# A list of steps in another order: the steps from the 120th on are re-ordered, and 117 of them change between VectorE and GpSimd

## The chip, the core and the metric

The kernel runs on one core of one Trainium2 chip. The metric is the device time of one execution in microseconds, as the median of several executions. In the profile the engines are called PE (TensorE, the matrix engine), DVE (VectorE), ACT (ScalarE), POOL (GpSimd) and SP (SyncE, which here issues the DMA transfers). All arithmetic is in 32-bit floats.

## The reference

The kernel computes a Mamba2 state-space layer and behind it a SwiGLU feed-forward layer. The first has batch 4, 8 heads, 768 positions, head dimension 32 and state 16, in 24 chunks of 32 positions:

```python
for c in range(nc):
    ...
    L = np.exp(cum[:, :, :, None] - cum[:, :, None, :]) * causal
    M = np.einsum('bhin,bhjn->bhij', Cc, Bc) * L
    y[:, :, sl] = np.einsum('bhij,bhjd->bhid', M, xc) \
        + np.einsum('bhin,bhnd->bhid', Cc, state) * np.exp(cum)[:, :, :, None]
    state = decay_full[:, :, None, None] * state + np.sum(Bx, axis=2)
```

Its result, as 3072 tokens of 256 numbers, goes through the second, with d_ff = 1536:

```python
xn = x / np.sqrt(np.mean(x * x, axis=-1, keepdims=True) + 1e-06) * rms_g
g = xn @ w_gate
return (g / (1.0 + np.exp(-g)) * (xn @ w_val) @ w_out).astype(np.float32)
```

## The kernel before

The 3072 tokens are cut into six blocks of 512. A block runs through the state-space layer (two pairs of chunk groups per block), the norm, the products with the gate and value weights, the product of SiLU(gate) and value (`hid`), and the product with the output weights. While PE makes the feed-forward products of one block, the other engines prepare the state-space part of the next.

Nothing is ordered by a scheduler. The program is a list of 1725 steps, written as one long string (`order`) at the end of the kernel. A loop reads it from the first to the last step and calls one small function for each; that function emits its instructions, each on a fixed engine. So the list sets the order on each engine, and each engine runs its own instructions in that order, waiting on semaphores for the others. A step reads `block:kind.numbers/banks`. A kind that ends in p (`hidp`, `hidgp`, `up`, `txp`, `cwp`, `twop`, `subp`, `scalep`, `scale2p`) is the same step on POOL instead of DVE.

The kinds that matter below, with the lines of the profile on which their instructions stand:

- `fetch.k` (L184): SP loads a piece of raw weights, 511.5 KB, into one of six buffers `wr`. `pow` (ACT), `man` (L224, DVE) and `wt` (L230, DVE) turn it into weights.
- `rowe` (L1196) stores decays to DRAM, `rowout` (L1189) row sums, `dT.p` (L566) loads the decays back, spread over partitions, and `Td.p` (L573, DVE) multiplies by them. `g` and `gg` (L592, L599, PE) are the products of C and B that come next; `L` and `L1` (L632 and on, DVE) multiply them by the decays, `y` (L705, L734, PE) are the layer's outputs.
- `spread` (L500, SP), `sub`/`subp` (L506) and `ex` make the decay matrix `L`; `ex` is an exponential on ACT and two causal selects on POOL (L493).
- `ms`, `rs`, `rb` are the sums and roots of the norm, `xn` (L873, DVE, two instructions) applies it; `tx`/`txp` (L954) make differences of it.
- `early` and `gate` (L901, L891, PE) are the first block's first feed-forward products. `P.k.j` (L977, PE) are the others: seven products for four, in the manner of Strassen; `take` (L983, ACT) and `C` (L989, DVE) combine them, `silu` is ACT's, `hid`/`hidp` (L1002) multiplies.
- `u.n`/`up.n` (L1076) are sums and differences of parts of `hid`, `cw` (L946) and `two` (L1054) the same of weights, for the output product `O.k.h` (L1108, PE), which uses 20 products with such sums. `w.n` (L1139, DVE, or ACT) adds its parts into `ob`, and `put` (SP) stores the result.

Of the kernel before, what the change touches and what calls it, by code (L numbers as in the profile page):

```python
# [20 lines left out]
def kernel(  # L21
# [1255 lines left out]
    def of_chunk(n, fn):  # L1277
# [45 lines left out]
        0:L1.2.2 0:fetch.8 0:fetch.9 0:silu.2 0:hid.2 0:man.8 0:pow.8 0:wt.8 0:L1.2.3 0:gate.3/2
        0:pow.7 0:gate.4/1 0:fetch.6 0:man.6 0:A.2 0:txp.0.1 0:silu.3 0:x.3 0:hid.3 0:pow.6
        0:gate.5/0 0:tx.0.2 0:txp.0.3 0:fetch.11 0:wt.7 0:man.9 0:fetch.10 0:S.2 0:silu.4 0:pow.9
        0:fetch.12 0:hid.4 0:bc.5 0:wt.6 0:cwp.3.0 0:wt.9 0:silu.5 0:hid.5 0:man.11 0:cw.3.1
        0:cw.3.2 0:cw.4.0 0:fetch.13 0:silu.1 0:y.2/2 0:S.3 0:x.5 0:cwp.4.1 0:ydone.0 0:switch.1
        0:P.2.3 0:bc.4 0:x.4 0:switch.0 0:pow.11 0:P.1.3 0:P.1.4 0:take.1.3 0:C.11.3 0:P.2.4 0:P.6.3
        0:yt.2 0:sq.2 0:gg.3/2 0:take.1.4 0:silug.11.3 0:C.11.4 0:L.3.0 0:take.6.3 0:cwp.3.3 0:P.5.3
        0:cwp.1.0 0:P.7.3 0:silug.11.4 0:P.6.4 0:take.7.3 0:P.5.4 0:P.4.3 0:hidgp.11.3 0:wt.11  # L1330
        0:L1.3.2 0:scale.5 0:L1.3.3 0:cwp.4.2 0:cwp.4.3 0:take.6.4 0:C.22.3 0:P.3.3 0:man.10
        0:scale.4 0:pow.10 0:wt.10 0:silug.21.3 0:cwp.5.0 0:cwp.5.1 0:hidg.11.4 0:P.7.4 0:take.7.4
        0:y.3/2 0:C.12.3 0:fetch.15 1:table 0:silug.22.3 0:hid.1 0:P.4.4 0:pow.12 0:silug.21.4
        0:hidg.21.3 0:spread.10 0:spread.9 0:P.1.5 0:spread.11 0:silug.12.3 0:C.22.4 0:P.2.5
# [6 lines left out]
        0:up.0 0:u.3 0:pow.15 0:wt.15 0:o.2 0:o.3 0:o.4 0:o.5 0:xn.1 1:P.2.0 1:P.1.1 1:P.1.0
        0:fetch.16 0:man.16 0:pow.16 0:sq2.2.1.3 0:sq2.2.1.0 0:sq2.2.1.2 0:tx.1.0 0:u.1 0:tx.1.2
        0:u.2 0:pow.17 0:wt.16 0:wt.17 1:twop.2 1:twop.1 1:two.0 1:cwp.2.2 0:O.16 0:O.2 0:O.0 0:oc.0
        0:silug.12.4 0:oc.1 1:take.1.0 0:C.12.5 0:tx.1.1 1:P.6.0 1:take.6.0 0:silug.12.5 1:C.11.0
        1:silu.11.0 0:O.4 1:P.5.0 1:two.3 1:two.8 1:two.11 1:two.9 0:tx.1.3 0:u.9 1:P.7.0 1:take.1.1
        1:P.6.1 0:O.15 0:ex.11 1:P.2.1 0:w.2 0:O.17 0:w.3 0:hidg.12.5 0:O.6 1:take.7.0 1:take.6.1
        1:P.7.1 1:C.11.1 1:P.5.1 1:silu.11.1 1:take.7.1 0:w.5 0:w.6 0:w.0 1:spread.0 1:spread.2
        0:sq2.2.1.1 1:two.5 1:T.0.1 1:twop.7 0:O.3 0:w.4 0:w.10 0:up.4 0:cwp.1.3 0:ydone.3 1:P.4.1
        1:silu.21.1 0:u.5 0:hidg.12.4 1:hid.21.1 1:C.22.0 0:w.1 1:hid.11.0 1:P.4.0 1:silu.21.0
        0:up.6 0:hidgp.22.5 0:u.7 0:up.8 1:cw.2.1 1:C.22.1 0:O.9 0:u.10 1:Tt.0.1 1:P.1.2 1:take.1.2  # L1350
        0:O.18 0:w.8 0:O.8 1:P.3.0 1:C.12.0 1:silu.12.0 1:hid.21.0 0:w.9 1:silu.22.1 1:P.6.2
        1:take.6.2 1:Tt.0.0 1:P.3.1 1:P.2.2 1:twop.4 0:O.7 0:up.13 1:hidp.22.1 1:twop.6 0:ex.9
        1:cwp.2.3 1:hid.11.1 0:w.7 1:two.10 0:u.11 0:u.12 0:O.13 1:T.1.1 0:w.20 1:Tt.1.1 0:w.14
        0:w.15 1:P.7.2 1:take.7.2 0:O.12 1:P.1.3 0:O.11 1:P.4.2 0:w.16 1:C.11.2 1:hid.12.0 0:w.13
        0:w.22 0:u.14 0:w.18 0:w.11 0:O.5 1:take.1.3 1:P.6.3 0:O.14 1:silu.11.2 1:Tt.1.0 1:spread.3
        0:spread.8 1:sub.3 1:ex.3 1:dT.1 0:sq2.2.0.1 0:sq2.2.0.3 3:bc.0 0:sq2.2.0.2 1:C.12.1 0:w.12
        1:T.0.0 1:hid.11.2 0:O.1 0:w.19 0:u.15 1:T.1.0 0:O.19 1:P.5.2 1:P.2.3 1:sq2.1.0 1:sq2.1.1
        1:dT.0 1:sq2.0.3 1:sq2.1.2 1:sq2.0.0 1:sq2.0.2 0:w.21 0:w.17 0:w.23 0:w.24 0:O.10 1:scale2.0
        0:w.25 0:put.2 1:spread.1 0:put.0 0:put.3 0:put.1 1:sq2.1.3 1:take.6.3 1:P.7.3 1:silu.21.2
        1:g 1:C.22.2 1:take.7.3 1:P.4.3 1:Td.1 1:C.11.3 0:sub.10 1:hid.21.2 1:silu.22.2 0:table.0  # L1360
        1:silu.12.1 1:hidp.12.1 1:silu.22.0 1:hidp.22.0 1:hidp.22.2 0:sub.8 1:P.3.2 1:C.12.2
        1:silu.11.3 1:silu.21.3 0:ex.8 1:P.1.4 1:take.1.4 0:ex.10 1:subp.2 1:hid.21.3 1:P.5.3
        1:C.22.3 1:P.2.4 1:C.11.4 1:silu.11.4 1:hid.11.4 1:P.6.4 1:take.6.4 1:silu.22.3 1:P.3.3
        1:P.1.5 1:silu.12.2 3:table 1:take.1.5 1:hidp.12.2 1:C.12.3 1:silu.12.3 1:P.7.4 1:take.7.4
# [12 lines left out]
        1:O.14.0 1:O.5.0 1:O.14.1 2:scale2.0 1:O.5.1 1:w.7 1:w.22 1:u.14 1:w.8 1:O.19.0 1:O.19.1
        1:u.15 1:O.10.0 1:O.10.1 1:xn 2:P.1.1 1:tx.0 1:txp.2 2:take.1.1 1:w.14 1:txp.1 1:w.25 1:w.19
        1:w.17 1:w.23 1:w.15 1:tx.3 1:w.24 2:Td.1 2:P.1.0 2:take.1.0 2:P.2.0 2:P.6.1 2:C.11.0
        2:P.6.0 1:ex.2 1:ex.0 1:ex.1 2:sq2.1.2 2:spread.2 2:sq2.0.0 2:sq2.0.3 2:sq2.0.1 2:spread.0  # L1380
        1:w.21 1:put.2 2:sq2.1.3 2:P.2.1 2:C.11.1 2:L1.3 2:take.6.1 2:P.7.1 2:take.6.0 2:P.7.0
        2:take.7.0 0:exps 2:P.5.0 2:L1.2 2:C.22.0 2:L 2:P.5.1 2:take.7.1 2:P.4.0 2:silu.21.0
        2:silu.11.1 2:silu.11.0 2:silu.22.0 2:hid.11.0 2:C.22.1 2:P.3.0 2:C.12.0 2:hid.21.0 2:P.4.1
        2:silu.21.1 2:hid.21.1 2:subp.3 2:ex.3 2:y 2:hidp.22.0 2:P.1.3 2:take.1.3 2:subp.0 2:sq
        2:P.1.2 2:take.1.2 2:P.3.1 2:C.12.1 2:silu.12.1 2:hid.11.1 2:hidp.12.1 2:P.6.3 2:P.2.2
        2:take.6.3 2:silu.22.1 3:T.1.1 2:C.11.2 2:P.2.3 2:C.11.3 2:sq2.0.2 3:T.1.0 2:silu.11.3
        2:P.6.2 2:take.6.2 2:P.7.3 2:hid.22.1 2:P.5.3 2:take.7.3 2:C.22.3 3:T.0.0 2:x.1 2:spread.1
        2:hid.11.3 3:Tt.1.1 2:silu.22.3 2:hidp.22.3 2:P.7.2 2:P.5.2 2:take.7.2 2:silu.11.2 2:C.22.2
# [130 lines left out]
```

## Time and profile before

| | |
|---|---|
| median of three runs | 387.2 us (386.33 to 387.54) |
| the profiled execution | 387.79 us, of which the span of instructions is 386.0 us |
| granted clock of TensorE | 1.00 |
| PE busy | 379.9 us, 98% of the span |
| DVE, ACT, POOL busy | 282.1, 219.7, 152.3 us |
| moved by DMA | 28.04 MB |

The share of an engine is its busy time over the span. A list of waits says for which producer an engine stood still, and the chain of waits follows the work that ended last backwards to its start. A row of a timeline gives the start, the busy time, the engine, the line, the instruction and its operands, and in brackets how long the engine idled ahead of it and who released it. Rows of equal instructions that follow each other are joined (x12).

### The profile page before, as it was taken

How to read it: one execution, taken by the hardware profiler on the slowest of the kernel's cores; microseconds unless marked ns; L12 is line 12 of the kernel's file. 1: busy time of each engine (PE TensorE's matmuls, PEld its weight loads, DVE VectorE, ACT ScalarE, POOL GpSimd, SP SyncE). 2: the span in 40 equal slices, each digit the busy share in tenths (PEclk: the TensorE clock that was granted, in tenths of full speed). 3: DMA queues.
4: the chain of work that ended last, by engine and by line, in shares of the span. 5: the costliest groups of instructions: out<-in, count | busy, mean ns of one | idle time of the engine just before them, and what ended most of it. 6: DMA issues, size and time to landing. Idle time of an engine off the chain costs nothing.

```text
span 386.0 us, 9707 instructions
## 1 busy us (share of the span) xinstructions
PE 379.9 (98%) x3837; PEld 330.1 (85%) x3837; DVE 282.1 (73%) x632; ACT 219.7 (57%) x455; POOL 152.3 (39%) x171
## 2 busy tenths in 40 slices
PE   8999999999999999999999999999999999999997
PEld 5675478889988999888898988899888899888996
DVE  6895979999997989656688566578735677454675
ACT  2778767957698361776571446562474551555410
POOL 5022046536756554553475501463630046112131
PEclk9999999999999999999999999999999999999999
...
DMA packets 110084, 28.04 MB, mean 73 GB/s; under 512 B 94840, under 2 KB 107992, under 8 KB 110040
## 3 DMA queue, kind: packets, MB, share of 16 engines
...
## 4 chain that ended last, share of the span: by engine, by line
PE 92%; DMA 3%; DVE 1%; SPq 1%; ACT 1%; issue 1%; DVEq 0%
PE gate L977 30%; PE o L1108 23%; PE val L977 22%; PE y L734 3%; PE gate L891 3%; PE o L1009 3%; PE g L599 1%; DMA rowe<-e_sb 1%; PE gate L901 1%; DMA dT<-rowe 1%; PE e L460 1%; PE g L592 1%; DMA L<-rowd 1%; SPq L143 0%; PE idle L328 0%
## 5 line engine op out<-in xcount | busy, mean ns | idle before, releaser
L989 DVE TENSOR_TENSOR c<-val,p 128x512 f32<-128x512 f32 x99 | 67.6, 687 | 39.1 <-PE val L977 30.3
L983 ACT COPY p<-gate 128x512 f32<-128x512 f32 x99 | 56.9, 582 | 49.7 <-PE gate L977 46.6
L977 PE MATMUL gate<-tx,wgv 128*128 128x256 f32 x264 | 65.8, 380 | 0.0
L977 PEld LDWEIGHTS gate<-tx,wgv 128*128 128x128 f32 x264 | 49.4, 190 | 6.7 <-ACT p L983 0.2
L1002 POOL TENSOR_TENSOR hid<-c 128x256 f32<-128x256 f32 x31 | 24.3, 795 | 76.4 <-ACT c L208 73.7
L208 ACT ACTIVATE c<-c 128x256 f32<-128x256 f32 x99 | 39.0, 414 | 25.4 <-DVE c L989 25.1
L1108 PE MATMUL o<-two,hid 128*128 128x128 f32 x308 | 42.4, 276 | 0.0
L1139 DVE TENSOR_TENSOR ob<-ob,o 128x128 f32<-128x128 f32 (+1 forms) x116 | 31.1, 295 | 14.0 <-PE o L1108 9.6
L1108 PEld LDWEIGHTS o<-two,hid 128*128 128x128 f32 x308 | 39.1, 192 | 1.1 <-ACT ob L1135 0.2
L1002 DVE TENSOR_TENSOR hid<-c 128x256 f32<-128x256 f32 x68 | 30.1, 455 | 7.9 <-ACT c L208 7.5
L977 PE MATMUL val<-tx,sw 128*128 128x256 f32 x132 | 33.9, 381 | 0.0
L977 PE MATMUL val<-xn,sw 128*128 128x256 f32 x132 | 33.9, 379 | 0.0
L977 PE MATMUL val<-xn,wgv 128*128 128x256 f32 x132 | 33.5, 380 | 0.0
L977 PE MATMUL gate<-xn,wgv 128*128 128x256 f32 x132 | 33.2, 381 | 0.0
L977 PE MATMUL gate<-tx,sw 128*128 128x256 f32 x132 | 33.1, 379 | 0.0
L1076 POOL TENSOR_TENSOR s<-s,hid 128x512 f32<-128x512 f32 (+1 forms) x14 | 18.1, 1291 | 28.3 <-PE o L1108 24.8
L493 POOL TENSOR_SCALAR_AFFINE_SELECT L<-L 64x512 f32<-64x512 f32 x32 | 22.0, 686 | 14.8 <-ACT L L208 13.7
L977 PEld LDWEIGHTS val<-xn,wgv 128*128 128x128 f32 x132 | 24.9, 190 | 3.4
L977 PEld LDWEIGHTS val<-tx,sw 128*128 128x128 f32 x132 | 24.6, 190 | 3.7 <-issue 0.4
L977 PEld LDWEIGHTS gate<-tx,sw 128*128 128x128 f32 x132 | 24.8, 190 | 3.2
L1002 DVE TENSOR_TENSOR hid<-u,gate 128x256 f32<-128x256 f32 x33 | 13.6, 417 | 18.5 <-ACT u L208 18.5
L1076 POOL TENSOR_TENSOR s<-hid 128x512 f32<-128x512 f32 (+1 forms) x15 | 19.6, 1310 | 18.5 <-DVE hid L1002 14.3
...
## 6 DMA issues: line engine op xcount, KB each, us to landing
...
wr<-in_moe_w_out_dram SPq DMA_DIRECT2D x6, 511.5 KB, 5.3
...
wr<-in_moe_w_gate_dram SPq DMA_DIRECT2D x5, 511.5 KB, 4.5
wr<-in_moe_w_val_dram SPq DMA_DIRECT2D x5, 511.5 KB, 5.6
...
```

Source lines behind the costliest of these rows:

```text
L208: nc.scalar.activation(**operands)
L493: nc.gpsimd.affine_select(out=L[r], in_=L[r], pattern=[[0, L.shape[1]], [1, HC]], compare_op=ALU.is_ge, fill=0.0, base=0, channel_multipli ...
L734: nc.tensor.matmul(out=y[2 * k + u][rows, (2 * n + i) * HC:(2 * n + i + 1) * HC], start=(k, u, rows.start) not in opened, stop=True, skip_ ...
L891: nc.tensor.matmul(out=gv[:, k], lhsT=w[:, t, fs], rhs=xns[0][:, t], start=(t == 0), stop=(t == 1))
L977: nc.tensor.matmul(out=dst[:, half[w]], lhsT=lhsT, rhs=rhs, start=(k in (1, 2, 5) and w == 0), stop=True, skip_group_check=True)
L983: nc.scalar.copy(out=t, in_=Xs[j])
L989: nc.vector.tensor_tensor(out=t, in0=Zs[j], in1=a, op=ALU.add)
L1002: engine.tensor_tensor(out=hid[:, 2 * j + c // 10 - 1, c % 10 - 1], in0=u, in1=src[:, half[1]], op=ALU.mult)
L1009: nc.tensor.matmul(out=o, lhsT=hid[:, f, k // 2, (k % 2) * P:(k % 2 + 1) * P], rhs=wo[:, f], start=opens, stop=(f == NF // 2 - 1), skip_gr ...
L1076: engine.tensor_tensor(out=hidden_or_sum(o)[:, g], in0=hidden_or_sum(in0)[:, g], in1=hidden_or_sum(in1)[:, g], op=ALU.add if in1[0] == "+" ...
L1108: nc.tensor.matmul(out=Os[blk, b][:, place * P:(place + 1) * P], lhsT=hidden_or_sum(u)[:, g], rhs=rhs, start=(blk, b) not in opened, stop= ...
L1139: nc.vector.tensor_tensor(out=o, in0=o, in1=src, op=ALU.add if what[0] == "+" else ALU.subtract)
```

## The change

Only the string `order` differs. The first 119 steps are the same; from the 120th on the same 1725 steps stand in another order, and 117 of them change their engine: 63 go from DVE to POOL (34 `hid`, 9 `u`, 5 `tx`, 4 `cw`, 4 `sub`, 6 `scale`, 1 `two`) and 54 from POOL to DVE (22 `u`, 16 `hid`, 7 `cw`, 5 `tx`, 2 `two`, 2 `sub`). The string is one line longer, so lines behind it move by one. Two lines of before and two of after:

```diff
-        0:early.1.0/1 0:early.1.1 0:dT.3 0:man.4 0:table.1 0:x.2 0:norm.1 0:man.5 0:Td.3 0:silu.0
...
-        2:O.13.0 2:O.13.1 2:ex.2 3:L 2:up.11 2:O.11.0 3:sq2.0.3 2:rb 2:xn 2:w.9 2:O.11.1 3:P.1.0
...
+        0:man.7 0:pow.4 0:wt.4 0:Tt.2.0 0:pow.7 0:fetch.9 0:fetch.8 0:dT.3 0:Td.3 0:wt.7 0:fetch.6
...
+        2:ex.2 3:L 3:L1.3 2:O.13.0 2:O.5.0 2:O.13.1 2:up.11 2:O.5.1 2:O.11.0 2:O.11.1 3:sq2.0.3 2:rb
```

On SP, in the first block, a piece of the difference from the store of the decays (`rowe.0`) to the loads of x:

```order
 L1196 DMA rowe<-e_sb 4x32x128
 L1189 DMA rowd<-r_sb 128x2x64
-L184 DMA wr<-in_moe_w_val_dram 128x2x1023
+L184 DMA wr<-in_moe_w_val_dram 128x2x1023 x2
+L184 DMA wr<-in_moe_w_gate_dram 128x2x1023
 L566 DMA dT<-rowe 128x1x256
-L150 DMA xr<-in_x_dram 128x8x32 x2
-L184 DMA wr<-in_moe_w_gate_dram 128x2x1023
-L184 DMA wr<-in_moe_w_val_dram 128x2x1023
```

Ahead of `dT.3` stood one load of weights; now there are three, `fetch.9` and `fetch.8` with it, and the loads of x have moved behind.

On POOL, at the end of block 2's feed-forward work, before:

```order
L1076 TENSOR_TENSOR s<-hid 128x512
L1076 TENSOR_TENSOR s<-s,hid 128x512
L493 AFFINE_SELECT L<-L 64x512 x4
L1002 TENSOR_TENSOR hid<-c 128x256
L493 AFFINE_SELECT L<-L 64x512 x2
L1076 TENSOR_TENSOR s<-s,hid 128x512
L954 TENSOR_TENSOR tx<-xn 128x256
```

And at the same place after:

```order
L1002 TENSOR_TENSOR hid<-c 128x256 x3
L1076 TENSOR_TENSOR hid<-s,hid 128x4x128
L493 AFFINE_SELECT L<-L 64x512 x6
L1076 TENSOR_TENSOR s<-s,hid 128x512
L954 TENSOR_TENSOR tx<-xn,tx 128x256
```

The `hid` between the selects (`hid.12.4`) has gone to DVE, and two sums that stood ahead of the selects with it; `up.11`, the `s` behind them, stays.

On DVE at that place, where the next block's `L` and the norm `xn` meet, before:

```order
L1076 TENSOR_TENSOR hid<-hid 128x4x128
L632 TENSOR_TENSOR L<-g,L 128x2x4x128
L873 SCALAR_TENSOR_TENSOR xn<-yt,gcol,sq 128x512 x2
L632 TENSOR_TENSOR L<-g_2657,L 128x4x128
L632 TENSOR_TENSOR L<-g_2658,L 128x4x128
```

And after:

```order
L1139 TENSOR_TENSOR ob<-ob,o 128x128
L632 TENSOR_TENSOR L<-g,L 128x2x4x128
L632 TENSOR_TENSOR L<-g_2663,L 128x4x128
L873 SCALAR_TENSOR_TENSOR xn<-yt,gcol,sq 128x512 x2
L632 TENSOR_TENSOR L<-g_2662,L 128x4x128
```

One of the two single `L1` steps now stands ahead of `xn`.

More of the change, by code (lines that the diff above doesn't have):

```diff
@@ L1323 @@
[L1323 to L1334, printed above, removed]
@@ L1341 @@
[L1341 to L1352, printed above, removed]
@@ L1353 @@
[L1353 to L1364, printed above, removed]
@@ L1377 @@
[L1377 to L1388, printed above, removed]
@@ L1389 @@
-        2:P.3.3 2:P.4.3 2:silu.21.3 2:C.12.3 2:silu.12.3 2:hidp.12.3 2:P.4.2 2:silu.21.2 3:T.0.1
-        2:hid.11.2 2:hid.21.3 3:Tt.0.0 2:P.3.2 2:hid.21.2 2:C.12.2 2:silu.12.2 2:hidp.12.2 2:subp.2
-        2:table 2:P.1.5 2:take.1.5 2:silu.22.2 2:P.1.4 2:take.1.4 2:P.2.5 2:C.11.5 2:hid.22.2
-        2:sub.1 1:put.3 1:put.1 3:dT.0 2:silu.12.0 3:Tt.0.1 3:Tt.1.0 3:Td.1 2:P.6.5 2:take.6.5
-        2:silu.11.5 2:P.6.4 2:take.6.4 2:P.2.4 2:C.11.4 2:hid.12.0 2:silu.11.4 2:P.7.5 2:take.7.5
-        3:sq2.1.3 2:x.0 3:spread.3 3:sq2.1.2 1:put.0 3:Td.0 2:scale2.1 2:hid.11.5 2:P.7.4 2:P.5.4
@@ L1473 @@
-        5:w.20 5:w.14 5:w.9 5:w.13 5:w.15 5:w.16 5:O.12.1 5:w.22 5:w.18 5:u.14 5:O.5.0 5:up.13
-        5:O.14.0 5:O.5.1 5:w.17 5:u.15 5:O.1.0 5:O.1.1 5:O.19.0 5:O.19.1 5:w.12 5:w.19 5:w.24 5:w.23
-        5:put.3 5:put.0 5:put.1 5:O.10.0 5:O.10.1 5:w.25 5:put.2.1 5:O.14.1 5:w.21 5:put.2.0
+        0:scale.3 0:eps 0:rowout.0 0:scalep.2 0:early.0.0/0 0:pow.2 0:pow.3 0:fetch.5 0:mask.2/2
+        0:parts.1 0:ms.0 0:rs.0 0:man.2 0:cwp.0.0 0:wt.2 0:wt.3 0:early.0.1 0:norm.0 0:sums.3
+        0:exp.3 0:sums.2 0:xn.0 0:txp.0.0 0:txp.0.1 0:tx.0.3 0:turn.2 0:T.2 0:Tt.2.1 0:man.4 0:Td.2
@@ new lines @@
+        0:turn.3 0:T.3 0:Tt.3.1 0:Tt.3.0 0:exp.2 0:early.1.0/1 0:early.1.1 0:norm.1 0:gate.2/0
+        0:man.7 0:pow.4 0:wt.4 0:Tt.2.0 0:pow.7 0:fetch.9 0:fetch.8 0:dT.3 0:Td.3 0:wt.7 0:fetch.6
+        0:x.2 0:man.5 0:silu.0 0:hid.0 0:man.8 0:gg.2/1 0:L.2.0 0:pow.5 0:wt.5 0:man.9 0:L1.2.2
+        0:L1.2.3 0:silu.1 0:pow.8 0:wt.8 0:hid.1 0:fetch.11 0:x.3 0:silu.2 0:hid.2 0:gate.3/2
+        0:silu.3 0:hid.3 0:ydone.0 0:man.6 0:A.2 0:S.2 0:pow.6 0:wt.6 0:cwp.3.0 0:cw.1.0 0:pow.9
+        0:wt.9 0:cwp.4.0 0:man.11 0:tx.0.2 0:pow.11 0:gate.4/1 0:silu.4 0:hid.4 0:switch.1
@@ new lines @@
+        0:gate.5/0 0:silu.5 0:hid.5 0:cw.1.2 0:y.2/2 0:cw.3.1 0:cw.3.3 0:S.3 0:cwp.3.2 0:bc.4
+        0:fetch.13 0:scale.4 0:switch.0 0:P.1.3 0:take.1.3 0:P.2.3 0:C.11.3 0:P.1.4 0:cw.4.2
+        0:cw.4.1 0:table.1 0:sq.2 0:yt.2 0:cwp.4.3 0:P.6.3 0:take.6.3 0:gg.3/2 0:L.3.0 0:take.1.4
+        0:fetch.10 0:fetch.14 0:man.10 0:wt.11 0:pow.10 0:wt.10 0:cwp.5.0 0:cwp.5.2 0:P.2.4 0:C.11.4
+        0:L1.3.3 0:P.7.3 0:P.6.4 0:P.5.3 0:take.7.3 0:P.4.3 0:C.22.3 0:silug.11.3 0:take.6.4 0:bc.5
+        0:scalep.5 0:fetch.12 0:pow.12 0:man.12 0:L1.3.2 0:spread.10 0:x.4 0:silug.11.4 0:silug.21.3
@@ new lines @@
+        1:cw.2.1 0:up.4 0:up.5 0:w.6 0:w.1 0:up.6 0:u.7 0:up.8 0:u.10 1:P.3.0 1:C.12.0 0:u.11
+        1:hid.11.1 1:T.1.1 0:O.18 0:w.7 0:O.8 1:silu.22.0 1:two.4 1:P.6.2 1:two.10 1:P.2.2 1:C.11.2
+        0:w.11 0:up.12 0:O.12 0:w.8 0:w.12 0:O.7 0:up.13 0:O.11 3:table 1:Tt.1.1 1:take.6.2 1:P.7.2
+        0:O.13 1:P.5.2 1:hid.21.0 0:w.13 0:up.14 0:w.20 0:w.9 0:w.15 0:w.14 0:w.22 1:silu.12.0
+        1:hidp.12.0 1:twop.6 1:hidp.22.0 0:ex.9 1:take.7.2 1:P.1.3 1:take.1.3 0:O.14 1:Tt.1.0
+        1:spread.3 1:sub.3 0:up.15 1:ex.3 1:spread.1 0:sq2.2.0.3 1:sq2.1.0 0:sq2.2.0.2 0:w.16
@@ new lines @@
+        0:ex.8 1:hid.12.1 1:g 1:P.1.4 1:take.1.4 1:P.5.3 1:P.2.4 1:C.22.3 1:C.11.4 1:Td.0
+        1:silu.22.3 1:silu.11.4 1:P.1.5 1:take.1.5 1:P.6.4 1:take.6.4 1:Td.1 1:P.3.3 1:C.12.3
+        1:P.5.4 1:hid.22.3 1:silu.12.3 1:hid.12.3 1:L1.2 1:P.7.4 1:take.7.4 1:C.22.4 1:P.6.5
+        1:take.6.5 1:silu.22.4 1:P.2.5 1:C.11.5 1:table 1:silu.11.5 1:sub.0 1:hidp.11.5 1:P.4.4
+        1:silu.21.4 1:hid.21.4 1:P.7.5 1:P.5.5 1:take.7.5 1:O.15.0 1:hidp.11.4 1:L 1:C.22.5
+        1:hidp.22.4 1:u.0 1:P.4.5 1:silu.21.5 1:O.2.0 1:O.2.1 1:w.0 1:hid.21.5 1:u.1 1:P.3.5 1:L1.3
@@ new lines @@
+        2:hid.11.3 2:hidp.22.1 2:P.5.3 2:P.7.2 2:take.7.2 3:dT.0 2:C.22.3 2:silu.22.3 2:hid.22.3
+        2:sq2.0.3 1:put.2 2:sq2.0.2 3:T.0.0 3:bc.0 2:spread.1 3:bc.1 2:spread.0 2:sq2.1.2 2:sq2.1.1
+        2:P.5.2 2:P.3.3 3:dT.1 1:put.3 2:C.22.2 2:silu.11.2 2:silu.22.2 2:silu.12.0 2:hidp.12.0
+        2:C.12.3 2:P.4.2 2:silu.21.2 2:hid.21.2 2:P.4.3 2:silu.21.3 2:hid.21.3 3:T.0.1 3:Tt.0.0
+        2:silu.12.3 2:hidp.12.3 2:P.3.2 3:T.1.1 2:C.12.2 2:sub.1 3:T.1.0 2:hid.22.2 2:P.1.5 3:Tt.0.1
+        2:take.1.5 2:silu.12.2 2:P.1.4 2:take.1.4 2:P.2.4 3:Tt.1.0 3:Tt.1.1 3:Td.1 2:P.6.5
@@ new lines @@
+        2:take.6.5 2:subp.0 2:hidp.12.2 2:x.1 3:spread.3 1:put.0 1:put.1 3:spread.0 2:P.6.4
+        2:take.6.4 2:sq 2:P.2.5 2:C.11.5 2:silu.11.5 2:hidp.11.5 2:C.11.4 2:P.7.5 2:take.7.5 3:Td.0
+        2:P.7.4 2:silu.11.4 2:take.7.4 2:table 2:hidp.11.2 2:hid.11.4 2:P.5.4 2:C.22.4 2:P.4.5
+        2:silu.21.5 2:hid.21.5 2:u.1 2:silu.22.4 2:hidp.22.4 2:P.4.4 2:silu.21.4 2:hid.21.4 2:P.5.5
+        2:C.22.5 2:yt 2:O.2.0 2:O.15.0 2:O.2.1 2:u.0 2:u.3 2:up.4 2:O.15.1 2:silu.22.5 2:w.2 2:w.0
+        2:u.2 2:P.3.5 2:C.12.5 2:silu.12.5 2:O.0.0 3:exps 2:O.3.0 2:hid.12.5 2:hid.22.5 2:O.3.1
@@ L1476 @@
+        5:w.18 5:w.7 5:put.0 5:O.5.0 5:O.5.1 5:w.17 5:u.15 5:put.3 5:O.1.0 5:O.1.1 5:O.19.0 5:O.19.1
+        5:w.12 5:w.19 5:w.23 5:put.1 5:O.10.0 5:O.10.1 5:w.24 5:w.25 5:put.2.1 5:O.14.0 5:O.14.1
+        5:w.21 5:put.2.0
     """
```

215 lines of the change are left out of this document (116 added, 99 removed).

## The prediction

> **What bounds the kernel now.** I read the head of the page first, then the list of waits of TensorE, then the chain of waits at the places that this list names, and last the timelines of the other engines there. The head gives the span and, for each engine, busy time, share and instructions:
>
> ```profile
> span 386.0 us, 9707 instructions
> PE 379.9 (98%) x3837; PEld 330.1 (85%) x3837; DVE 282.1 (73%) x632; ACT 219.7 (57%) x455; POOL 152.3 (39%) x171
> ```
>
> PE is busy for 98% of the span. DVE at 73% and POOL at 39% have room on the average, so they matter only where PE stands still for them. The list of PE's waits (us in total, times, longest) shows where:
>
> ```profile
> PE idle L328 <- DVE warm L354: 1.1, 1, 1.1
> PE g L599 <- DVE T L573: 0.7, 1, 0.7
> PE y L705 <- DVE S L686: 0.5, 1, 0.5
> PE o L1108 <- POOL s L1076: 0.4, 1, 0.4
> PE y L734 <- DVE L L632: 0.2, 1, 0.2
> ```
>
> The first and the third belong to the start of the program (the warm-up and the first outputs y.0), inside the 119 steps that the change leaves alone. What a new order can take away is the other three: 0.7 + 0.4 + 0.2 = 1.3 us. As a second count, the windows view from 22 us to the end, with PE's busy time behind the length, and the end of the chain:
>
> ```profile
> 22.00:386.00 364.00, 359.80 (x3587) 316.46 (x3585) 264.82 (x580) 206.56 (x431) 146.19 (x153) 1.00 0.31 67
> ```
>
> ```profile
> 375.95 7.24 PE o L1108 x64
> ...
> 383.22 0.29 DVE ob L1139
> ```
>
> PE's last product ends at 375.95 + 7.24 = 383.2. PE idles 364.00 - 359.80 = 4.2 us there. Of these 386.0 - 383.2 = 2.8 us lie behind its last product: the addition w.21, then the store put.2.0 and its landing. The new table ends with the same two steps, so this tail stays. 4.2 - 2.8 = 1.4 us are left for gaps, which agrees with 1.3 from the waits. The granted clock there is 1.00, so nothing is to be had from the clock. Both tables issue the same matrix products in the same shapes, so PE's busy time stays at about 380 us. **The gain is therefore at most 1.4 us (0.36%), and the loss has no such lid:** PE has no slack in which a new stall could be taken back.
>
> **Place A, 26 to 38 us: two weight loads ahead of dT.3.** The chain of waits (start, us, what) runs here over DMAs:
>
> ```profile
> 28.98 4.52 DMA rowe<-e_sb
> ...
> 33.55 3.35 DMA dT<-rowe
> ...
> 36.99 0.44 DVE T L573
> ```
>
> rowe.0 stores the decays, dT.3 loads them back spread out, Td.3 multiplies by them on DVE, and the products gg.2 go on behind it. PE's own rows (start, busy, then the wait) say what that costs today:
>
> ```profile
> 36.27 0.46 PE L599 MATMUL g<-T 32*64 32x128 f32 x12
> 37.47 0.65 PE L599 MATMUL g<-T 32*64 32x128 f32 x20 [0.74 <-DVE T L573]
> ```
>
> PE is ready at 36.27 + 0.46 = 36.73 and stands for 0.74 us. Anything that makes dT.3 land later adds to that one for one. Before the change SP issues in this order:
>
> ```profile
> 26.20 0.43 SPq L184 DMA_DIRECT2D wr<-in_moe_w_gate_dram  x1
> 26.68 0.47 SPq L184 DMA_DIRECT2D wr<-in_moe_w_val_dram  x1
> 28.25 0.63 SPq L566 DMA_DIRECT2D dT<-rowe  x1
> 28.98 0.55 SPq L1196 DMA_DIRECT2D rowe<-e_sb  x1
> 29.63 0.43 SPq L1189 DMA_DIRECT2D rowd<-r_sb  x1
> 30.11 0.47 SPq L184 DMA_DIRECT2D wr<-in_moe_w_val_dram  x1
> 33.55 0.60 SPq L566 DMA_DIRECT2D dT<-rowe  x1
> ```
>
> The change puts two more loads of raw weights (fetch.9 and fetch.8) between the last two rows. SP stands there until rowe.0 has landed at 28.98 + 4.52 = 33.50. Two of the six raw buffers have been read out by then, so the two loads will be issued at about 30.6 and 31.1, half a microsecond apart as those of 26.20 and 26.68 are, ahead of dT.3. How much they delay it I take from three rows. The DVE rows of the two multiplications show when each dT landed (each starts 0.09 us behind the landing, by the chain's 33.55 + 3.35 = 36.90 and 36.99):
>
> ```profile
> 33.11 0.42 DVE L573 TENSOR_TENSOR T<-tp,dT 128x256 f32<-128x256 f32 x1 [2.43 <-DMA dT<-rowe]
> 36.99 0.42 DVE L573 TENSOR_TENSOR T<-tp,dT 128x256 f32<-128x256 f32 x1 [1.49 <-DMA dT<-rowe]
> ```
>
> dT.2, of the same size, was issued at 28.25 behind two such loads (26.20 and 26.68) and landed at 33.02, so it took 4.77 us. dT.3, issued when the one load ahead was 3.4 us old, took 3.35. The difference is 1.4 us. The other way is to count room. This is the DMA view from 25 to 40 us in slices of 0.375 us, busy tenths and GB/s, with the size and time of one load:
>
> ```profile
> DMA  6999534579999998898899530025999992898999
> GB/s 60 91 114 112 51 71 113 132 246 316 338 349 371 409 366 314 280 210 183 253 379 409 201 120 33 16 66 179 221 201 194 163 124 67 278 311 327 398 387 398
> ...
> wr<-in_moe_w_val_dram SPq DMA_DIRECT2D x4, 511.5 KB, 5.2
> ```
>
> While loads run (28.4 to 30.6 us) they move 316 to 409, on average 358 GB/s, so two loads of 511.5 KB need 1023/358 = 2.9 us. The idle slices from 33.25 to 35.1 us (busy 5, 3, 0, 0, 2) are worth 4.0 slices or 1.5 us. What does not fit in them, 1.4 us, stands ahead of dT.3. Both ways give +1.4 us. The ends are 0 (dT.3 overtakes the loads, or they fill only the gap) and +2.9 (nothing fits). **I take +1.4.** That it cannot be below 0: dT.3 still waits for the same rowe.0, which sits ahead of the two loads in the queue as before.
>
> [...] No row here shows a DMA passing one ahead of it in SP's queue.
>
> On DVE, the hid and the weight sums queued behind Td.3 start later too, but PE's next products after gg.2 read only xn and wgv. On SP nothing is issued later than today except the loads of x, which come behind one load of weights more; their reader y.2 is far off.
>
> What the two loads gain by being earlier: their conversions on ACT and DVE come sooner, but no wait of PE in the list is for a weight. I cost it at nothing.
>
> **Place B, 200 to 208 us: the boundary from block 2 to 3.** The rows of POOL, PE and DVE:
>
> ```profile
> 201.59 0.72 POOL L1002 TENSOR_TENSOR hid<-c 128x256 f32<-128x256 f32 x1
> 202.27 1.86 POOL L493 TENSOR_SCALAR_AFFINE_SELECT L<-L 64x512 f32<-64x512 f32 x2
> 204.21 1.27 POOL L1076 TENSOR_TENSOR s<-s,hid 128x512 f32<-128x512 f32 x1
> ```
>
> ```profile
> 203.06 2.05 PE L1108 MATMUL o<-two,hid 128*128 128x128 f32 x16
> 205.53 1.16 PE L1108 MATMUL o<-two,s 128*128 128x128 f32 x8 [0.42 <-POOL s L1076]
> ...
> 208.05 0.77 PE L734 MATMUL y<-T,S 32*64 32x64 f32 x48 [0.22 <-DVE L L632]
> ```
>
> ```profile
> 204.16 1.22 DVE L632 TENSOR_TENSOR L<-g,L 128x1024 f32<-128x1024 f32 x1 [0.55 <-POOL L L493]
> 205.30 1.40 DVE L873 SCALAR_TENSOR_TENSOR xn<-yt,gcol,sq 128x512 f32<-128x512 f32 x2
> ```
>
> POOL is late by one hid of 0.72 us that stands between its causal selects. In the new table that hid.12.4 is DVE's, and the selects follow each other. So the last selects may start at 201.59 and end by 203.5, and the sum s (up.11) by 204.8, against PE's need at 203.06 + 2.05 = 205.1: the wait of 0.42 goes. DVE, which waited 0.55 us for these selects, gives about as much for the hid (0.455 us on DVE, below) and starts L some 0.6 us sooner. What is late next: DVE now runs one L1 between L and xn. L from 203.5 to 204.7, L1 to 205.35 (half of an L), then the first half of xn to 206.05; PE, 0.42 us earlier than today, wants xn at about 206.1. That is tight, as is the second L1, which y waits for. The ends are 0 and the whole -0.6 (0.42 + 0.22); **I take -0.5.**
>
> **The rest of the moved work.** The 117 flips are all sums, differences and products between SBUF tiles, and DVE and POOL pay for them like this (count, us, mean ns, idle before):
>
> ```profile
> L1002 DVE TENSOR_TENSOR hid<-c 128x256 f32<-128x256 f32 x68 | 30.1, 455 | 7.9 <-ACT c L208 7.5
> L1002 POOL TENSOR_TENSOR hid<-c 128x256 f32<-128x256 f32 x31 | 24.3, 795 | 76.4 <-ACT c L208 73.7 <-issue 2.5
> ```
>
> 34 hid go to POOL and 16 come back, so POOL gains 18 x 0.8 = 14 us and DVE loses 18 x 0.455 = 8 us. Of the sums (s), 9 go to POOL and 22 come back: 13 x 1.3 = 17 us less for POOL, 13 x 0.72 = 9 us more for DVE. The shares stay near 73% and 39%, and nothing of it is on PE's path unless it comes late at one place. Two rows show that DVE's price for a sum depends on what POOL does:
>
> ```profile
> 191.15 0.69 DVE L1076 TENSOR_TENSOR hid<-hid 128x512 f32<-128x512 f32 x1 [1.25 <-POOL s L1076]
> 194.87 1.18 DVE L1076 TENSOR_TENSOR s<-s,hid 128x512 f32<-128x512 f32 x1
> ```
>
> The first ran beside an idle POOL, the second beside POOL's own sum: 0.5 us more. At the boundary from block 1 to 2 the new table has one of POOL's tx behind six selects (two of them took 1.86 us at 202.27), where POOL's tx stood ahead of them, and several boundaries now have four products between y and the norm's sums instead of five. Ends: -0.2 (the rest of the 1.4) and +2 (four boundaries with one 0.5 us each). I take +0.2, one short wait, since the list shows that four of five boundaries wait for nothing today.
>
> **Sum.** 1.4 - 0.5 + 0.2 = +1.1 us. Against the profiled execution (387.8 us, with 386.0 of span and 1.8 around it) that is 388.9. That execution is 0.6 us above the median of the three runs, so by the median it is 387.2 + 1.1 = **388.3 us**. About 0.3% (1.2 us) is what a measurement of this kernel can tell from no change.
>
> **Rivals.** *One: dT.3 is not late.* If the two loads move at the 409 GB/s of the best slice, they are 1023/409 = 2.5 us of work. 1.5 us of it fit in the gap, 0.3 us in the four slices at 8 tenths from 30.6 to 32.5, and the 0.7 us over would have to run beside dT.3, in whose own slices only 179 to 221 GB/s move. Then A costs nothing. It decides from the point where dT.3 lands by 36.9. Then only B counts: 387.2 - 0.5 = 386.7, and 385.8 if all of the 1.4 us goes. For it: the gap is really empty (busy 0). Against it: dT.2's 4.77 us behind two loads. This one ends on the other side, not slower. *Two: the engines get in each other's way at a boundary.* With the sums on DVE beside POOL's hid, three or four instructions ahead of xn at a boundary cost 0.5 us more each, and PE, without slack, waits 1.5 to 2: 388.3 + 1.8 = 390.1. For it: the 1.18 against 0.69 us, and xn is already tight at B. Against it: DVE waited at these places itself (0.55, 1.25 us). [...] *Three: nothing of it is on the path*, A fills the gap and B's gain is taken by xn: 387.2.
>
> **Chances.** The forecast 0.50: its own range, 387.9 to 389.2, lies on both sides of the 388.4 from which it is slower; slower 0.26, same 0.24. Rival one 0.28: faster 0.12 (it needs nearly all of the 1.4 us), same 0.16. Rival two 0.17: slower. Rival three 0.05: same. Together faster 0.12, same 0.45, slower 0.43. The range reaches into rival one (386.4 is its 386.7 with a third of a microsecond more) and just past rival two (390.2).
>
> **What would show it.** Step A: in the changed profile dT<-rowe issued at about 33.5 lands near 38.3, Td.3 starts near 38.4, and the wait of PE g L599 for DVE T grows from 0.7 to about 2.1. Step B: the wait of PE o L1108 for POOL s is gone, and no wait of gate for xn replaces it at 204 to 207 us. The rest: the list of PE's waits holds at most one new entry under 0.5 us, and PE's busy time stays at 380 us. I am wrong if dT.3 takes 3.4 us or less behind two loads, or if a boundary shows a new wait over 1 us.

## The result, and the profile after

The changed kernel takes 391.2 us (median of four runs, 389.05 to 392.99); the kernel before took 387.35 us in the same comparison (386.33 to 387.54). The ratio is 1.0101, with a 95% interval of 1.0074 to 1.0128: slower by 3.9 us, where +1.1 was forecast and 390.2 was the end of the range. Ratios here and below leave out executions more than 1.5% longer than the fastest of the same kernel.

The head of the page after, and its clock in 40 slices of 9.7 us:

```profile
span 389.2 us, 9695 instructions
PE 380.9 (98%) x3837; PEld 330.5 (85%) x3837; DVE 284.3 (73%) x623; ACT 214.8 (55%) x451; POOL 149.2 (38%) x180
...
PEclk9999899999999999999999999999999999999999
```

DVE, ACT and POOL are busy nearly as before (within 5 us each). One slice of the clock, from 39 to 49 us, is not at 9. The list of PE's waits:

```profile
PE g L599 <- DVE T L573: 3.1, 1, 3.1
PE idle L328 <- DVE warm L354: 1.1, 1, 1.1
PE y L705 <- DVE S L686: 0.5, 1, 0.5
PE y L734 <- issue: 0.4, 1, 0.4
```

The two waits of place B (0.4 and 0.2 us) are gone, and the one of place A has grown from 0.7 to 3.1 us. PE's rows, SP's issues and the chain of waits show how:

```profile
35.65 0.46 PE L599 MATMUL g<-T 32*64 32x128 f32 x12
39.25 0.71 PE L599 MATMUL g<-T 32*64 32x128 f32 x20 [3.14 <-DVE T L573]
```

```profile
29.45 2.09 SPq L184 DMA_DIRECT2D wr<-in_moe_w_val_dram  x2
31.59 0.46 SPq L184 DMA_DIRECT2D wr<-in_moe_w_gate_dram  x1
32.15 0.60 SPq L566 DMA_DIRECT2D dT<-rowe  x1
```

```profile
32.15 6.59 DMA dT<-rowe
...
38.77 0.44 DVE T L573
```

dT.3 takes 6.59 us behind the loads, against 3.35 before. It is issued 1.4 us earlier in this execution (32.15 against 33.55), since PE's work in the unchanged first steps already ran 0.62 us ahead (the same two products started at 10.00 us before and at 9.38 after), and since rowe.0, issued at 28.32, had landed within 3.8 us, where it took 4.52 before. The two rows of the start, before and after:

```profile
10.00 0.38 PE L481 MATMUL e<-sel,row 32*128 32x512 bf16 x2
```

```profile
9.38 0.38 PE L481 MATMUL e<-sel,row 32*128 32x512 bf16 x2
```

The windows view shows what the stall did to PE afterwards. The columns are the window, its length, busy time of PE, PEld, DVE, ACT and POOL, then the granted clock, the DMA share and GB/s:

```profile
38.00:39.00 1.00, 0.00 (x0) 0.00 (x0) 0.23 (x1) 0.97 (x3) 0.00 (x0) 1.00 1.12 278
39.00:40.00 1.00, 0.75 (x21) 0.52 (x21) 1.00 (x3) 0.53 (x1) 0.00 (x0) 0.86 1.25 177
40.00:41.00 1.00, 1.00 (x2) 0.48 (x3) 1.00 (x4) 0.18 (x1) 0.00 (x0) 0.50 0.54 51
41.00:42.00 1.00, 1.00 (x3) 0.48 (x2) 1.00 (x3) 0.42 (x1) 0.00 (x0) 0.50 0.74 252
42.00:43.00 1.00, 1.00 (x2) 0.44 (x2) 0.96 (x4) 0.00 (x0) 0.00 (x0) 0.50 1.13 327
43.00:44.00 1.00, 1.00 (x3) 0.38 (x2) 1.00 (x4) 0.00 (x0) 0.00 (x0) 0.93 1.28 190
```

Half a microsecond after PE comes back, its clock falls to one half, for 3.4 us (39.72 to 43.13). That costs 0.14 + 3 x 0.50 + 0.07 = 1.7 us, and PE counts as busy all the while. So the profiled pair adds up: +2.4 us of stall, +1.7 of clock, -0.6 at place B, +0.4 for the wait marked issue, -0.6 for the start: +3.3, where the spans differ by 389.2 - 386.0 = 3.2 us. Between executions the clock's part varies: the four runs show a mean clock of 0.996, 0.996, 0.991 and 0.991, which is up to 1.6 us lost in the first two and up to 3.5 us in the others (less where PE stands while the clock is low), and the two at 0.991 are the longest (391.49 and 392.99).

### The profile page after: what moved, and what is told of

Same layout as the page of the kernel before. It is cut to its first block, busy times and chain, and to the rows that moved or that the text cites. A ratio compares the mean times of both kernels' runs of the same rounds, so it can differ in the third digit from the quotient of the medians.

```text
span 389.2 us, 9695 instructions
## 1 busy us (share of the span) xinstructions
PE 380.9 (98%) x3837; PEld 330.5 (85%) x3837; DVE 284.3 (73%) x623; ACT 214.8 (55%) x451; POOL 149.2 (38%) x180
## 3 DMA queue, kind: packets, MB, share of 16 engines
q1 hardware_dynamic: 107960, 27.30, 33.4%
## 4 chain that ended last, share of the span: by engine, by line
PE 96%; DMA 2%; DVE 1%; issue 0%
PE gate L977 29%; PE o L1108 26%; PE val L977 22%; PE gate L891 3%; PE y L734 3%; PE o L1009 3%; PE gate L901 2%; DMA dT<-rowe 2%; PE g L599 2%; PE e L460 1%; PE g L592 1%; PE tp L540 1%; PE e L474 0%; PE idle L328 0%; PE As L664 0%
## 5 line engine op out<-in xcount | busy, mean ns | idle before, releaser
L1002 POOL TENSOR_TENSOR hid<-c 128x256 f32<-128x256 f32 x49 | 38.0, 784 | 83.9 <-ACT c L208 79.5
L1139 DVE TENSOR_TENSOR ob<-ob,o 128x128 f32<-128x128 f32 (+1 forms) x116 | 30.7, 296 | 14.5 <-PE o L1108 12.8
L977 PE MATMUL gate<-tx,sw 128*128 128x256 f32 x132 | 33.4, 380 | 0.0
L1002 DVE TENSOR_TENSOR hid<-c 128x256 f32<-128x256 f32 x50 | 25.4, 512 | 7.5 <-ACT c L208 7.5
L977 PEld LDWEIGHTS gate<-xn,wgv 128*128 128x128 f32 x132 | 24.3, 190 | 3.2 <-DVE hid L1002 0.2
L977 PEld LDWEIGHTS val<-xn,sw 128*128 128x128 f32 x132 | 24.3, 191 | 3.0
L208 ACT ACTIVATE u<-gate 128x256 f32<-128x256 f32 (+1 forms) x37 | 14.9, 402 | 20.0 <-PE gate L977 12.7
```

What stands on the lines that cost most here:

```text
L208: nc.scalar.activation(**operands)
L977: nc.tensor.matmul(out=dst[:, half[w]], lhsT=lhsT, rhs=rhs, start=(k in (1, 2, 5) and w == 0), stop=True, skip_group_check=True)
L1002: engine.tensor_tensor(out=hid[:, 2 * j + c // 10 - 1, c % 10 - 1], in0=u, in1=src[:, half[1]], op=ALU.mult)
L1139: nc.vector.tensor_tensor(out=o, in0=o, in1=src, op=ALU.add if what[0] == "+" else ALU.subtract)
```

## The experiments

The theory: the two loads ahead of dT.3 make PE stand at gg.2, and that stall makes the clock fall. The rivals: the rest of the new order or the flips cost the time; or the clock falls for another reason. An execution is one measured run of a kernel; only one of each kernel has a profile. Each time is set against runs of the kernel before on the same chip, whose medians lay between 386.4 and 386.9 us.

**The edit undone (late_fetch).**

```diff
-0:fetch.9 0:fetch.8 0:dT.3 0:Td.3
+0:dT.3 0:fetch.9 0:fetch.8 0:Td.3
```

> The changed order with one edit: the two weight loads fetch.9 and fetch.8 stand behind dT.3 again instead of ahead of it. Theory (the two loads delay dT.3, PE then stands 3.1 us at gg.2, and a stall of that length halves the granted clock for some 3 us): dT.3 takes 3 to 4 us, the wait of PE g L599 for DVE T falls from 3.1 to under 1 us, the granted clock is 1.00 throughout, and the time is 386.5 to 387.5 us, near the kernel before. Rival (the loss of 3.9 us comes from the rest of the new order and the 117 flips): the time stays above 389.5 us.

387.7 us, ratio 1.0027 (1.0007 to 1.0048): three quarters of the loss are gone, but the time is just above the range expected, and five of twelve executions show a clock of 0.996. The wait at gg.2 is gone too, but another stands 6 us later. The waits of PE, the DVE row behind it, PE's row and two windows with the clock:

```profile
PE A_ps L664 <- DVE L L644: 2.1, 1, 2.1
```

```profile
39.67 0.43 DVE L224 TENSOR_SCALAR m<-wr 128x512 int32<-128x512 uint32 x1 [2.35 <-DMA wr<-in_moe_w_gate_dram]
```

```profile
42.19 0.63 PE L664 MATMUL A_ps<-xr,Bd 64*32 64x64 f32 x24 [2.07 <-DVE L L644]
```

```profile
44.00:46.00 2.00, 2.00 (x4) 0.90 (x3) 1.84 (x7) 1.97 (x4) 0.00 (x0) 0.50 1.25 143
46.00:48.00 2.00, 2.00 (x5) 0.76 (x5) 1.97 (x5) 1.93 (x4) 0.79 (x1) 0.80 0.94 265
```

The new order has the reader of fetch.8 (man.8) on DVE ahead of the multiplications of gg.2's products by the decays (L.2 and L1.2). With the load later, man.8 holds DVE up for 2.35 us, PE stands for 2.07 and the clock halves again, from 43.4 to 46.8 us.

**The edit alone, in the order of before (early_fetch).**

```diff
-0:dT.3 0:man.4
+0:fetch.9 0:fetch.8 0:dT.3 0:man.4
...
-0:L1.2.2 0:fetch.8 0:fetch.9 0:silu.2
+0:L1.2.2 0:silu.2
```

> The order of before with one edit: fetch.9 and fetch.8 are moved ahead of dT.3, as in the changed order; nothing else. Theory: the whole loss appears, the wait of PE g L599 for DVE T grows from 0.7 to about 3 us, the granted clock falls to 0.5 for some 3 us behind it, and the time is 390.5 to 392 us (the changed kernel's loss without its gain of 0.6 us at the boundary). Rival (the rest of the new order costs the time): 386.5 to 388 us.

390.35 us, ratio 1.0109 (1.0079 to 1.0140): the whole loss, from two steps moved. In the profiled execution dT.3 took 6.03 us and PE stood for 1.88, less than the 3 us expected:

```profile
32.28 6.03 DMA dT<-rowe
```

```profile
38.88 0.65 PE L599 MATMUL g<-T 32*64 32x128 f32 x20 [1.88 <-DVE T L573]
```

There the clock stayed at 1.00 and the run took 389.7 us; four of the six runs show a mean of 0.990 to 0.995.

**PE kept at work in the stall (filled).** Two of the four products of gate.2 are made twice:

```diff
-0:man.8 0:gg.2/1
+0:man.8 0:again.2 0:gg.2/1
```

> The changed order with extra work for PE ahead of gg.2: two of the four products of gate.2 are made a second time (same result, about 1.7 us), so that PE stands still for about 1.4 us instead of 3.1; dT.3 lands as late as before. Theory (the length of the stall sets the clock): the granted clock stays 1.00, and the time falls by about 1.7 us to 389.5, although PE has more to do. Rival (the clock falls for another reason, or its fall is not on the path): no change from 391.2, or slower.

388.3 us, ratio 1.0045 (1.0023 to 1.0067): with 1.8 us more work for PE, the loss is 2.2 us smaller than the changed kernel's (0.0056 of 387). One of the twelve executions, 393.15 us at a clock of 0.991, is not in this ratio; with it the difference would be about 1.8 us. PE's rows:

```profile
36.25 1.88 PE L1244 MATMUL gate<-xn,wgv 128*128 128x512 f32 x4
38.06 0.79 PE L599 MATMUL g<-T 32*64 32x128 f32 x32
```

In this execution dT.3 came sooner than in the changed kernel's profile (Td.3 starts at 37.72 us, there at 38.77), so no stall was left, and the gain can't be put down to the filling alone; the clock was 1.00 or 0.999 in ten of twelve runs.

**The stall alone, without the loads (stalled9, stalled6, stalled4).** The order of before, with memsets on DVE ahead of Td.3:

```diff
-0:man.5 0:Td.3
+0:man.5 0:spin.9 0:Td.3
```

> The order of before, its DMAs untouched, with nine extra memsets of 128x512 on DVE (0.4 to 0.5 us each) ahead of Td.3; DVE idled there for 1.5 us, so Td.3 comes 2.2 to 3 us later and PE stands for 3 to 3.7 us at gg.2. Theory (a stall of PE of that length is enough): the clock falls to 0.5 for some 3 us behind it, and the time rises by the extra stall plus about 1.7 us, to 391 to 392. Rival (the clock falls because of the DMA traffic or of what stands around it in the new order): the clock stays 1.00 and the time is 389.5 to 390.3, the stall alone.

393.9 us, ratio 1.0193 (1.0173 to 1.0213), and a mean clock of 0.990 or 0.991 in all five runs. The stall was longer than meant: the memsets, 0.48 us each, start 0.66 us apart, and ahead of each of the last eight DVE idles for 0.17 us with the memset before it as the releaser. PE's wait:

```profile
PE g L599 <- DVE T L573: 5.1, 1, 5.1
```

5.1 - 0.7 = 4.4 us of it are new. The clock is at one half from 38.91 to 45.74 us, twice 3.41 us, but PE stands until 41.01, so the half clock costs it 4.73 x 0.5 = 2.4 us; together 6.8, where 7.0 were measured. With six memsets:

> As the run with nine memsets, with six: there each took 0.66 us with its wait for the one before and PE stood for 5.1 us, so six should give a stall of about 3.1 us, the length in the changed kernel, with the DMAs of before. Theory: +2.4 us of stall and about 1.6 us of half clock, 390 to 391 us, with a mean clock of 0.99 to 0.997 in most executions, as in the changed kernel. Rival (the changed kernel's clock fell by its DMA traffic): +2.4 us and clock 1.00.

390.5 us, ratio 1.0106 (1.0077 to 1.0135). The stall was 2.1 us in the profile, not 3.1, and the clock fell in four of six runs (0.996 three times, 0.991 once). PE's row and a window:

```profile
38.08 0.65 PE L599 MATMUL g<-T 32*64 32x128 f32 x20 [2.11 <-DVE T L573]
```

```profile
40.00:42.00 2.00, 2.00 (x4) 0.85 (x3) 1.97 (x5) 1.97 (x3) 0.00 (x0) 0.50 1.09 168
```

With four:

> The same with four memsets: a stall of about 1.8 us, 1.1 us longer than before. If the fall of the clock needs a stall above a fixed length between 1.9 us (no fall in the profile of the run with the early loads) and 2.1 us (a fall in the run with the late loads), the clock is 1.00 in all executions and the time is +1.1 us, 387.6 to 388.0. If it depends on where the stall falls in time, some executions show 0.995 and 1.6 us more, and others 1.00.

387.7 us, ratio 1.0036 (1.0019 to 1.0053). In the profiled execution the stall was 0.7 us, as without memsets; two of eleven runs show 0.996, and they are the slowest (389.46 and 390.42). So a stall is enough, with the DMAs of before. Whether the clock falls does not go by the stall's length alone: a stall of 1.9 us left it at 1.00 in the profile of early_fetch, and it fell behind 2.1 us in those of stalled6 and late_fetch and behind 1.7 us in that of late_both. More on that stands under place A below.

**Loads and their readers late (late_both).** As late_fetch, with man.8 and man.9 moved behind L.2 and L1.2:

> The changed order with the two loads fetch.9 and fetch.8 behind dT.3 and, besides, their readers on DVE (man.8 and man.9) behind the three multiplications L.2 and L1.2; in the run with the loads alone moved, man.8 waited 2.4 us for its load and held up these multiplications, and PE stood 2.1 us for them at A_ps. Theory (the two stalls with the fall of the clock behind them are the whole loss; the rest of the new order is worth -0.6 us): neither wait is left, the granted clock is 1.00, and the time is 0.3 to 0.6 us below before, 386.3 to 386.6. Rival (something else in the new order costs 1 us or more too): 387.5 or above.

386.8 us, ratio 1.0015 (0.9993 to 1.0036). The median is level with before; the profiled execution, at 389.75 us the slowest of twelve, shows the next in line. The loads of x now stood behind three weight loads:

```profile
41.95 0.91 PE L664 MATMUL A_ps<-xr,Bd 64*32 64x64 f32 x24 [1.71 <-DMA xr<-in_x_dram]
```

```profile
42.00:44.00 2.00, 1.88 (x26) 1.03 (x27) 2.00 (x5) 1.06 (x3) 0.00 (x0) 0.61 0.79 262
```

**And x ahead of them (x_first).** Also 0:x.2 straight behind 0:dT.3:

> As the run with both loads and their readers moved, and with the loads of x (x.2) ahead of the two weight loads too, straight behind dT.3, since in that run PE stood 1.7 us for x. Theory: no wait of PE of more than 0.5 us is left between 30 and 60 us, the granted clock is 1.00 in nearly every execution, and the time is 0.3 to 0.5 us below before, about 386.0. Rival (one more queue takes the place of the last, since the loads must run some time): another wait of over 1 us and 387 us.

386.4 us, ratio 0.9998 (0.9984 to 1.0013), the clock at 1.00 in all twelve runs. The time lies between theory (386.0) and rival (387). A wait over 1 us was left all the same, as the rival said, since hid.4 and hid.5 stand behind the conversions of the late weights on DVE:

```profile
51.24 1.13 PE L977 MATMUL gate<-xn,wgv 128*128 128x256 f32 x4 [1.40 <-DVE hid L924]
```

**And those ahead (hid_first).** gate.4 to hid.5 put before pow.9 and wt.9:

> As the run with x first, with gate.4, silu.4, hid.4, gate.5, silu.5 and hid.5 put ahead of the conversions of the late weights (pow.9, wt.9 and what follows), since hid.4 and hid.5 stood behind these on DVE and PE waited 1.4 us for the bank that they free. Theory (the late weights are the only thing wrong in the new order, and the rest is worth the 0.6 us of the waits at the boundary): no wait between 30 and 60 us is left, and the time is 0.5 to 1.2 us below before, ratio 0.997 to 0.9985. Rival (the rest of the new order is worth nothing, since other waits such as the one marked issue at 164 us take it back): ratio 0.999 to 1.001.

388.8 us, ratio 1.0054 (1.0033 to 1.0075), a miss by both sides; two of six executions show a clock of 0.994 and 0.995, the profiled one among them. The wait is gone, and two others that belong to the work pushed back have come:

```profile
52.48 1.10 PE L977 MATMUL gate<-tx,sw 128*128 128x256 f32 x4 [1.05 <-DVE sw L946]
...
54.88 0.85 PE L599 MATMUL g<-T 32*64 32x128 f32 x32 [1.30 <-ACT yt L827]
```

**One load ahead, one behind (one_late).**

```diff
-0:fetch.9 0:fetch.8 0:dT.3
+0:fetch.9 0:dT.3 0:fetch.8
```

> The changed order with one edit: fetch.9 stays ahead of dT.3, fetch.8 goes behind it. If each load ahead costs the same, dT.3 takes about 5 us (3.4 with neither ahead, 6.6 with both), PE waits 1 to 2 us at gg.2 or at A_ps for man.8, and the time lies between the kernel with both moved and the changed one, 388 to 390 us. If the delay sets in with the second load, dT.3 takes 3 to 3.5 us and nothing is waited for at gg.2.

387.4 us, ratio 1.0018 (0.9997 to 1.0039), below the 388 to 390 of the first case, although dT.3 was late as it says. dT.3 took 5.65 us with one load more ahead, against 3.35 in before's profile and 6.0 to 6.6 with two; the clock fell in one run of twelve.

```profile
31.14 5.65 DMA dT<-rowe
```

```profile
37.29 0.65 PE L599 MATMUL g<-T 32*64 32x128 f32 x20 [0.68 <-DVE T L573]
```

This profile has no wait of PE beside this one and the two of the unchanged start, and its span, 384.6 us, is 1.4 below that of before, place B's 0.6 among it. But single runs range from 384.7 to 389.1 us.

**The edit the other way round (fetch7_late).** In the order of before, fetch.7 from ahead of dT.2 to behind dT.3 and x.2:

> The order of before with one weight load, fetch.7, moved from ahead of dT.2 to behind dT.3 and x.2: the changed kernel's edit the other way round. Theory (each load ahead on SP's queue delays a small transfer by about 1 us or more): rowe.0 and dT.3 land 1 us or more sooner, the wait of 0.7 us at gg.2 goes, and the time is 0.5 to 0.7 us below before. Rival (the wait turns into one for the weights of fetch.7, or for another load behind it): no change, or a new wait of PE for a weight or for x.

386.5 us, ratio 1.0002 (0.9990 to 1.0014). The mechanism holds, the gain doesn't show. gg.2 runs without a wait, and other waits of 0.3 to 0.5 us stand in the list:

```profile
35.42 0.73 PE L599 MATMUL g<-T 32*64 32x128 f32 x32
```

```profile
PE r_ps L388 <- issue: 0.5, 1, 0.5
...
PE gate L977 <- DVE tx L954: 0.3, 1, 0.3
PE y L734 <- issue: 0.3, 1, 0.3
```

**The flips and the order apart (flips_only, order_only).** The order of before with the engines of after, and the reverse:

> The order of before, with the 117 steps on the engines that the changed kernel gives them. Theory (the flips alone cost or save little, since PE has its waits from the loads): 386.5 to 387.7 us, the wait at gg.2 stays at 0.7 us. Rival (DVE and POOL hold each other up, and a new wait at a block boundary appears): 388 to 390 us with a wait of over 1 us in the list of PE's waits.

419.9 us, ratio 1.0865 (1.0821 to 1.0909), a miss by both sides, by about 30 us. The longest waits are of the output products (O), and the mean clock of the profiled execution is 0.988. The first four rows of the list:

```profile
PE o L1108 <- POOL hid L1076: 4.6, 2, 3.4
PE o L1108 <- DVE ob L1139: 4.3, 2, 3.8
PE o L1108 <- DVE s L1076: 3.4, 1, 3.4
PE o L1108 <- POOL s L1076: 3.2, 2, 2.2
```

> The changed order, with the 117 steps on the engines of before. Theory: the loss of the changed kernel stays, since the two loads stand ahead of dT.3: a wait of about 3 us at gg.2, a clock under 1.00 and 390 to 392 us; work left on the engine for which the order was not made may add some tenths. Rival (the flips are the loss): 387 to 388 us.

410.3 us, ratio 1.0623 (1.0594 to 1.0652), a miss by both sides too, with a wait of only 1.0 us at gg.2. Neither half stands without the other. The flips are no small change, but in the full change the order pays for them: the list of after has none of these waits.

**One flip of place B (hid_flip).** hid.12.4 of block 2 on DVE:

> The order of before with one flip: hid.12.4 of block 2 goes from POOL to DVE. Theory (place B of the prediction): POOL's selects end about 0.7 us sooner, the wait of PE o L1108 for POOL s (0.4 us) goes from the list, and so does, or nearly, the 0.2 us of y for DVE L. Rival (DVE is then late itself): a wait of PE for DVE of the same size stands there instead.

One execution alone, 387.0 us, so only its list of waits counts here. The rival was right: the sum is late on DVE instead, by more.

```profile
PE o L1108 <- DVE hid L1076: 0.9, 1, 0.9
```

## Why the prediction was wrong

**What bounds it, and the lid on the gain: right.** PE's work and its share of 98% did not move, and no version came out measurably below before.

**Place A: the mechanism right, the size wrong, and the clock left out.** Two steps failed: the count of room, and the clock at nothing. The first mis-sized term is the delay of dT.3: +1.4 us, where the profiled execution shows 3.14 - 0.74 = +2.4. The count of room took the two loads as 2.9 us long, with 1.5 us of them in the empty slices of before. The DMA view of after, from 25 to 40 us in slices of 0.375 us:

```profile
DMA  9995829999999977699846989999999998999999
GB/s 89 123 105 86 100 82 300 360 371 387 387 404 407 317 214 164 142 323 339 333 186 136 207 224 300 262 327 377 382 379 371 379 347 248 299 291 292 227 185 130
```

From 32.5 to 33.25 us there still is a hollow (4 and 6 tenths). The two loads were issued by 31.5 and at 31.6, not at 30.6 and 31.1, and dT.3 0.56 us behind the second. The trace's DMA packets have sizes of their own, 2046 bytes for weights and 1024 for dT. Counted off in the order of the queue, 256 to a load, fetch.5's packets run from 30.7 to 33.4 us, those of the two loads from 33.4 to 36.8, and dT.3's from 36.1 to 38.0 (in before, behind fetch.5 alone, from 34.9 to 36.0). So dT.3's packets moved behind nearly all of the two loads', and these took 3.4 us, not 2.9. The empty slices of before, 0.62 us earlier on this execution's clock, are those from 32.6 to 34.5; the loads used them only from 33.4 on, for 1.1 us. By this estimate 3.4 - 1.1 = 2.3 us stood ahead of dT.3.

The size differs between executions: in early_fetch's profile the same two loads lengthened the wait by 1.88 - 0.74 = 1.1 us. The other way to the +1.4, dT.2's delay, had two loads ahead; here fetch.5 was a third. Behind one load dT.3 took 3.35 us in before (2.9 in late_fetch), behind two 5.65 (one_late), behind three 6.0 to 6.6 (early_fetch, filled, after). The end of the range, +2.9, did hold the delay. Rival one (dT.3 not late) is out by the same numbers.

The second term was missing. "The granted clock there is 1.00, so nothing is to be had from the clock" treats the clock as given. In these runs it went with PE's own stalls, and 1.7 us of the loss in the profiled execution are its fall. In the stall runs it fell with before's DMAs (in five of five executions of stalled9, four of six of stalled6); filled, in which PE works through the wait, shows it less often (two of twelve, where after has four of four). Stall and clock together, 2.4 + 1.7 = 4.1 us, are slightly more than the measured +3.9.

The traces show more of the fall. It lasts 3.41 us in after (39.72 to 43.13), 3.4 in late_fetch, late_both, stalled6 and hid_first, and 6.83, twice 3.41, in stalled9. Ahead of a fall the records of the clock in two traces show full clock for whole multiples of 3.413 us: in after from 5.59 to 39.72 us, 10 times, in before from 6.85 to 385.73, behind PE's last product, 111 times. Of the 3.41 us that end where the fall begins, PE stood for 1.7 us in late_both, 1.89 in hid_first, 2.07 in late_fetch, 2.1 in stalled6, 2.94 in after and 3.01 in stalled9. The author's estimate from these numbers is that the sum of PE's idle time within one such stretch decides; no run was made to test it. In hid_first, stalls of 1.05 and 1.30 us together were enough (window, length, PE's busy time and, third from the end, the clock):

```profile
51.89:55.30 3.41, 1.52 (x34) 1.10 (x36) 3.27 (x11) 2.23 (x8) 0.72 (x1) 1.00 0.91 251
55.30:58.71 3.41, 3.41 (x31) 2.55 (x13) 3.41 (x8) 2.02 (x4) 0.84 (x2) 0.50 0.72 138
```

In early_fetch, 1.88 us were not. Divided at 38.09 us, they lie in two stretches; that a stretch ends there is the author's estimate, which no row of the profile shows:

```profile
34.68:38.09 3.41, 2.32 (x17) 0.79 (x15) 0.39 (x1) 2.33 (x4) 0.00 (x0) 1.00 0.83 201
38.09:41.51 3.42, 2.63 (x25) 1.47 (x26) 3.07 (x7) 1.96 (x4) 0.00 (x0) 1.00 0.90 214
```

Single stalls of 1.71 (late_both), 2.07 (late_fetch) and 2.11 us (stalled6) were followed by the fall, and order_only's profile has one of 2.7 us at a mean clock of 0.999.

**Costing what the earlier loads gain at nothing was wrong as a reading of the order.** The new order leans on them: in the profiles, moved back alone they cost 2.1 us at A_ps, then 1.7 us for x, then 1.4 us for hid. With two moves (late_both) the time is no longer measurably above before, with three (x_first) the clock stays at 1.00 in all twelve executions, and the next shift (hid_first) costs again. Only one of the two loads moved back (one_late) is level with before too.

**Place B: right in the full change** (-0.6 us, both waits gone in the list), but for a reason only half named: the single flip of hid.12.4 gives the wait to DVE (0.9 us). The gain needs more of the new order than this flip; which part was not tested.

**The rest, +0.2 us: near in size by luck, wrong in its reason.** The only new short wait of after is the 0.4 us marked issue, and executions of before's order show it as well (0.5 in early_fetch, 0.6 in stalled4). "Nothing of it is on PE's path unless it comes late at one place": the flips alone are late at many and cost 33 us; the order that comes with them takes that away.

**Rival two** gave a time near the measured one (390.1) by a mechanism that the profile of after doesn't show: it has no wait over 0.5 us at a boundary; its time is no merit. What this part leaves open: why x_first, without the loss and with place B's gain, is level with before. Its profile has the 1.40 us above and a wait marked issue of about 1 us in the y products; whether these are in its other runs isn't known; the profiled execution, 388.2 us, is the slowest of the twelve.
